# Clustered attention with a Fourier and feed-forward layer: scales in PSUM, joint sign images, the maximum's pass in place, column folds on VectorE

## The chip, the cores and the metric

The kernel runs on one core of one Trainium2 chip. A core has five engines that run their own instruction queues: TensorE (PE; its weight loads are shown as PEld), VectorE (DVE), ScalarE (ACT), GpSimd (POOL) and SyncE (SP, which issues the DMAs). The metric is the time of one execution on the device in microseconds. Before the change three runs gave 1049.66, 1053.15 and 1053.73 us; their median is 1053.15 us.

## The reference

Four sequences (batch 4) of 768 tokens, 8 heads of 64. Queries and keys are each assigned to the nearest of 16 centroids; a query attends only to keys of its own cluster. The attention's output becomes the input `x` (4 x 768 x 512) of a layer that mixes with a Fourier transform and then applies a feed-forward network.

```python
mask = q_assign[:, :, :, None] == k_assign[:, :, None, :]
scores = np.where(mask, scale * q @ k.T, -1e9)
scores = scores - np.max(scores, axis=-1, keepdims=True)
attn = np.exp(scores) / (np.sum(np.exp(scores), axis=-1, keepdims=True) + 1e-9)
x = attn @ v                                   # heads side by side: 4 x 768 x 512
mixed = np.real(np.fft.fft(np.fft.fft(x, axis=1), axis=2))
u = x + mixed
un = (u - mean(u)) / np.sqrt(var(u) + 1e-6)    # over the 512 columns
out = u + np.maximum(un @ w_ch1, 0.0) @ w_ch2  # 512 -> 2048 -> 512
```

## The kernel before

Float32 operands are split into two 16-bit parts, a high one and the rest, and each product is made of three 16-bit matmuls. So besides PE's matmuls there is much splitting work on ACT (the high part), DVE or POOL (the rest).

**Attention** (class `Attention`) goes over 16 pairs of heads, four pairs per sequence, and in each pair over six tiles of 128 queries (`scores`, then `attend` two tiles later). For one tile and each head of the pair, PE makes scores of 128 x 768 in a two-bank PSUM tile `ps_big` (L320, with the cluster mask added at L325). DVE makes one pass over them (L339): it multiplies by a column `ne` (the negative scale) and takes the minimum along the row into `m`; the product itself goes to a destination `ju`. ACT makes the exponential (L343 or L345) with `m` as its bias, casts it to 16 bit (L353), POOL subtracts for the rest (L354), a DMA transposes both (`pt`), and PE multiplies with the values into `ps_o` (L374 to L376). `finish` divides on DVE (L386 to L390) and writes into `X`, the layer's input.

Here the first sequence (four pairs, `early`) differs from the other three. In the first, the product goes to a piece of `X[1]` and the exponential reads it from there with a constant scale of -1 (L343). In the other three the product goes to a 16-bit scratch tile `ju` that nobody reads, and the exponential reads the scores again from PSUM with the scale as a column `e` (L345).

**Weights** (class `Weights`) are split once, beside the first sequence's attention. There are 32 pieces of 128 x 512, 16 for each matrix, loaded as raw bytes through eight buffers. Per piece: `largest` takes the maximum of the upper half words (DVE, L491), `signs` makes two 16-bit images with ACT, one of the positive and one of the negative values (L519, L520), `join` adds them on PE into PSUM (L528) and puts the low bits back (DVE, L532), `halve` splits into high and low part. `signs` of a piece runs one step ahead of its `join`, `largest` three steps. The PSUM tiles of `psf` are a ring of three banks that the weights share with the attention's preparation, the Fourier and the feed-forward stages. For each group of four pieces, `scales` calls `top_power`: four operations of DVE on one column (first matrix, through `block`) or four columns (second matrix), L58 to L61, which turn a maximum into a power of two `s` and its inverse `inv`. Their operands lie in SBUF.

**Fourier** (class `Fourier`): `fold` uses the symmetry of the transform. For a difference and for a sum it adds rows (L660, DVE), then mirrored columns (L661: POOL for the difference, which comes first; DVE for the sum), splits the result and transposes it by DMA. It also folds one middle row on POOL (L654, L655), which `rest` transposes on PE later (L678 to L681). `transform` makes the matmuls.

**Feed-forward** (class `FeedForward`): `norm`, `up` (L858) and `down` (L888), the largest part of PE's work.

**Order.** `Overlap.run` lists what is done in which of some hundred time steps; PE's order is the program's. The layer of sequence b runs as a generator beside the attention of sequence b + 1: `fill` takes so much of it per tile that a budget of cost is used up, and the last sequence's layer runs alone. On the other engines a planner with a model of the costs orders the instructions at build time, so their order can change wherever a cost or a dependence changes.

Of the kernel before, what the change touches and what calls it, by code (L numbers as in the profile page):

```python
# [24 lines left out]

P = 128
B, H, S, D = 4, 8, 768, 64
NC_ = 16
ST = S // P
DM = H * D  # L30
DF = 4 * DM
SH = S // 2
# [19 lines left out]
FLOOR = float(2.0 ** -38)  # L52


def top_power(nc, tops, s, inv):

    t = tops.bitcast(I32)
    nc.vector.tensor_scalar(out=t, in0=t, scalar1=20, scalar2=None, op0=ALU.logical_shift_right)  # L58
    nc.vector.tensor_scalar(out=t, in0=t, scalar1=-910.0, scalar2=1.0, op0=ALU.add, op1=ALU.max)
    nc.vector.tensor_scalar(out=inv.bitcast(I32), in0=t, scalar1=240.0, scalar2=float(1 << 23), op0=ALU.min, op1=ALU.mult)  # L60
    nc.vector.reciprocal(out=s, in_=inv)  # L61
# [20 lines left out]
class Attention:  # L82
# [226 lines left out]
    def scores(self, pr, st):  # L309
        nc, sb = self.nc, self.sb  # L310
        assert self.ready >= pr
        (hq, hk), oh, (e, ne) = self.hl[pr], self.oht[pr], self.sc.scores(pr)
        sl = slice(st * P, (st + 1) * P)
        ps = [self.psum().rearrange("p (h x) -> p h x", h=2) for _ in range(2)]
        rows = [slice(D * j, D * (j + 1)) for j in range(2)]
        for hf in range(2):
            hs = slice(hf * SH, (hf + 1) * SH)
            for i, (a, c) in enumerate(((0, 0), (1, 0), (0, 1))):
                for j in range(2):
                    nc.tensor.matmul(out=ps[j][:, hf, 0:SH], lhsT=hq[rows[j], a, sl], rhs=hk[rows[j], c, hs],  # L320
                                     start=(i == 0), stop=False)
        for hf in range(2):
            for j in range(2):
                rz = slice(D * j + 32 * hf, D * j + 32 * hf + 32)
                nc.tensor.matmul(out=ps[j][:, hf, 0:SH].rearrange("p (s x) -> p s x", x=P), lhsT=oh[rz, st % 3 * 2 + st // 3],  # L325
                                 rhs=oh[rz, ST:], start=False, stop=True)
        for j in range(2):

            m = sb.tile([P, 1], F32, name="rmx", tag="rmx", bufs=6)
            early = pr < H // 2  # L330
            if early:

                n = (2 * st + j) % self.RING * S
                p32 = self.X[1].rearrange("p a x -> p (a x)")[:, n:n + S]
            else:
                p32 = sb.tile([P, S], F32, name="p32", tag="p32", bufs=2)
            x = p32.rearrange("p (h x) -> p h x", h=2)
            ju = x if early else sb.tile([P, 2, SH], BF16, name="ju", tag="ju")
            self.mark = nc.vector.tensor_scalar(out=ju, in0=ps[j][:, :, 0:SH], scalar1=ne, scalar2=None, op0=ALU.mult, op1=ALU.min,  # L339
                                    accum_out=m)  # L340
            self.late = m
            if early:
                nc.scalar.activation(p32, p32, AF.Exp, bias=m, scale=-1.0)  # L343
            else:
                nc.scalar.activation(x, ps[j][:, :, 0:SH], AF.Exp, bias=m, scale=e)  # L345
            if early and j:
                ph = sb.tile([P, S], F32, name="p32", tag="p32", bufs=2).bitcast(F16).rearrange("p (a x) -> p a x", a=2)
            else:
                ph = sb.tile([P, 2, S], F16, name="ph", tag="ph", bufs=2)
            if early and j and (st in self.PC):  # L350
                nc.gpsimd.tensor_copy(out=ph[:, 0], in_=p32)
            else:
                nc.scalar.copy(out=ph[:, 0], in_=p32)  # L353
            nc.gpsimd.tensor_tensor(out=ph[:, 1], in0=p32, in1=ph[:, 0], op=ALU.subtract)  # L354
# [79 lines left out]
class Weights:  # L434
# [6 lines left out]

    RAW, PN = tuple(4128 * i for i in range(6)) + (29696, 33824), (24768, 26816)
    ID, TOP, MX = 28864, 29376, 29472
    X32 = 37952, 40000
    EXTRA, A2, AHEAD = 0, 9, 7

# [51 lines left out]
    def block(self, g):  # L498

        nc, at = self.nc, self.arena.at  # L500
        mx = at(self.MX + 32 * (g % 2), [P, 4], F32)
        ps = self.psf()
        along(nc, ps[:, 0:P], mx[:, 0:1], self.ident)
        nc.vector.tensor_reduce(out=mx[:, 1:2], in_=ps[:, 0:P], op=ALU.max, axis=AX.X)
        self.scales(g, mx[:, 1:2])

    def scales(self, g, mx):
        n = mx.shape[1]
        s = self.sb.tile([P, 4], F32, name="wsc", tag="wsc", bufs=2)
        top_power(self.nc, mx, s[:, 0:n], self.inv[0][:, g:g + 1] if n == 1 else self.inv[1][:, 4 * (g - 4):4 * (g - 3)])  # L510
        for i in range(4):
            self.scale[4 * g + i] = s[:, i % n:i % n + 1]

    def signs(self, k):

        nc, at = self.nc, self.arena.at
        pn = at(self.PN[k % 2], [P, 2, DM], BF16)
        top = self.top(k)
        nc.scalar.activation(pn[:, 0].bitcast(I16), top.bitcast(I16), AF.Relu, bias=self.off[:, 0:1], scale=8.0)  # L519
        nc.scalar.activation(pn[:, 1].bitcast(I16), top, AF.Relu, bias=self.off[:, 1:2], scale=8.0)  # L520
        self.bits[k] = pn
# [99 lines left out]
class Fourier:  # L621
# [8 lines left out]

    CS, SS = (33888, 30816, 20480), (35456, 32352, 22016)
    FOLDS = ((1, ALU.subtract), (0, ALU.add))
    FE = (0, 0, 0, 1)
    UE = (1, 1, 1, 1)

    def __init__(self, tc, X, arena, psf, con, ident, sc):
# [10 lines left out]
    def fold(self, b):  # L647
        nc, at, X = self.nc, self.arena.at, self.X[b % 2]
        W, M = SH + 1, DM // 2
        self.tables()  # L650
        self.scale[b] = self.sc.sequence(b)
        s = self.scale[b][0]
        mid = at(self.XM, [1, M + 1], F32)
        nc.gpsimd.tensor_copy(out=mid, in_=X[0:1, 3, 0:M + 1])  # L654
        nc.gpsimd.tensor_tensor(out=mid[:, 1:M], in0=mid[:, 1:M], in1=X[0:1, 3, DM - 1:M:-1], op=ALU.add)  # L655
        last = at(self.XL, [P, 3], F32)
        xt = {}
        for i, op in self.FOLDS:
            f = at(self.XF, [P, 3, DM], F32)
            self.engine(self.FE[i]).tensor_tensor(out=f, in0=X[:, 0:3], in1=X[:, 3:6], op=op)  # L660
            self.engine(self.FE[2 + i]).tensor_tensor(out=f[:, :, 1:M], in0=f[:, :, 1:M], in1=f[:, :, DM - 1:M:-1], op=op)  # L661
# [239 lines left out]
class Overlap:  # L901
# [21 lines left out]
    MIX3 = (0, 0, 0, 0, 0, 0, 0, 1, 1, 1)  # L923
    F2 = 1
    PIN, PF, PV = (), 29, 1
    CE, WP, WQ = 0.45, 0, 0

    def layer(self, b, old):
        fft, ffn = self.fft, self.ffn
        mix = iter(self.MIX3 if b == B - 1 else self.MIX)  # L930
        for t in fft.transform(b):
            if t == "first":
                with self.tc.high_priority():
                    m = ffn.norm(b, 0)
                ffn.inverse(*m)
                continue
            yield 0.8 if t is None else None
            for _ in range(next(mix)):
                c = next(old, 0.0)
                if c:  # L940
                    yield c
        yield from old
        for blk in range(3):
            for f, cost in enumerate(ffn.up(blk)):
                if blk == 0 and f == 0:
# [171 lines left out]
```

## Time and profile before

| | us |
|---|---|
| median of three runs | 1053.15 |
| the profiled execution | 1049.91 |
| its span (first to last instruction) | 1048.1 |
| PE busy | 910.8 (87%) |
| DVE busy | 627.4 (60%) |
| ACT busy | 625.3 (60%) |
| POOL busy | 586.9 (56%) |

Busy time is the time in which an engine has an instruction under way. A view of groups has the line, engine and operation, the output's and the input's names and shapes, the count, then busy time and the mean in ns of one, then the engine's idle time just before, with what ended it. A view of waits says which line waited for which, with the total in us, how often, and the longest. The first sequence's attention with the weights lies in about the first 220 us; the last sequence's layer, alone, in about the last 150.

### The profile page before, as it was taken

What the parts mean: (1) busy time and instruction counts of PE and PEld (TensorE: products, weight loads), DVE (VectorE), ACT (ScalarE), POOL (GpSimd) and SP (SyncE); (2) the same over time, 40 slices, a digit from 0 to 9 for tenths busy, and PEclk for the clock granted to TensorE, in tenths of its full rate; (3) what the DMA queues carried; (4) which work ended last, traced back from release to release, by engine and by line L of the source; (5) the groups of instructions that cost most, each with busy time, mean ns of one, the idle gap of its engine ahead of it and who ended that gap; (6) DMA issues with size and microseconds to landing.
All of it is one profiled execution on the core that took longest, in us unless ns stands there. A gap on an engine that the chain in (4) does not pass through costs nothing.

```text
span 1048.1 us, 23542 instructions
## 1 busy us (share of the span) xinstructions
PE 910.8 (87%) x9350; PEld 591.7 (56%) x9362; DVE 627.4 (60%) x1297; ACT 625.3 (60%) x980; POOL 586.9 (56%) x693
## 2 busy tenths in 40 slices
PE   3665565749899999998899999997999999999998
PEld 2333333425575756655666757555757667576674
DVE  8789899767757555668656555667555333631110
ACT  4798889755766665645666746556756543351230
POOL 2364565753975756655856646647847645271230
PEclk9987878769899999999899999998999999999999
DMA  7799998979887776568877767588757562321000
GB/s 272 179 225 245 196 239 166 171 156 153 177 123 153 128 154 121 121 137 161 153 137 142 140 128 132 110 141 170 124 102 133 96 110 43 81 52 31 11 11 21
DMA packets 396239, 140.01 MB, mean 134 GB/s; under 512 B 381784, under 2 KB 381792, under 8 KB 396128
## 3 DMA queue, kind: packets, MB, share of 16 engines
q1 hardware_dynamic: 396128, 138.50, 65.9%
q8 instruction: 73, 1.20, 0.5%
q14 instruction: 38, 0.31, 0.1%
HBM read 42.52 MB, written 6.29 MB: 47 GB/s over the span
## 4 chain that ended last, share of the span: by engine, by line
PE 39%; DVE 6%; DMA 3%; ACT 3%; POOL 2%; issue 2%; SPq 0%; ACTq 0%; DVEq 0%; POOLq 0%
PE ps_f L888 16%; PE ps_f L858 13%; PE ps_big L320 3%; DMA pt<-ph 3%; PE ps_f L713 2%; DVE ju L339 1%; ACT p L345 1%; PE ps_o L374 1%; POOL ph L354 1%; PE ps_o L375 1%; PE ps_o L376 1%; PE ps_big L325 1%; ACT ph L353 1%; DMA scr<-in_k_dram 0%; DVE arena L660 0%
## 5 line engine op out<-in xcount | busy, mean ns | idle before, releaser
L354 POOL TENSOR_TENSOR ph<-p,ph 128x768 f16<-128x768 f32 x144 | 242.9, 1688 | 184.6 <-ACT ph L353 150.1
L858 PE MATMUL ps_f<-arena,w1h 128*128 128x256 f16 x1536 | 271.4, 277 | 19.1 <-ACT arena L866 9.0
L888 PE MATMUL ps_f<-w2h,arena 128*128 128x512 f16 x768 | 238.9, 379 | 0.0
L345 ACT ACTIVATE p<-ps_big,rmx,sce 128x768 f32<-128x768 f32 x144 | 142.1, 988 | 132.9 <-DVE ju L339 127.5
L858 PE MATMUL ps_f<-arena,w1l 128*128 128x256 f16 x768 | 212.4, 277 | 0.0
L339 DVE TENSOR_SCALAR_CACHE_REDUCE ju<-ps_big,sce 128x768 bf16<-128x768 f32 x144 | 146.1, 1014 | 68.2 <-PE ps_big L325 58.2
L888 PEld LDWEIGHTS <-arena 128*128 128x128 f16 x1152 | 108.7, 98 | 126.6 <-issue 5.2
L858 PEld LDWEIGHTS <-w1h 128*128 128x128 f16 x1536 | 152.1, 99 | 36.0 <-issue 14.3
L867 POOL TENSOR_TENSOR arena<-arena 128x256 f16<-128x256 f32 x192 | 128.1, 677 | 77.3 <-ACT arena L866 73.6
L320 PE MATMUL ps_big<-hlk,hlq 64*128 64x384 f16 x1152 | 128.9, 348 | 39.0 <-ACT p L345 23.4
L374 PE MATMUL ps_o<-v,pt 128*128 128x66 f16 x1152 | 124.8, 198 | 43.0 <-DVE X L390 27.5
L888 PE MATMUL ps_f<-w2l,arena 128*128 128x512 f16 x384 | 145.5, 379 | 0.0
L374 PEld LDWEIGHTS <-pt 128*128 128x128 f16 x1152 | 110.2, 100 | 57.7 <-issue 37.1
L353 ACT CAST ph<-p 128x768 f16<-128x768 f32 x144 | 119.6, 832 | 15.0 <-DMA pt<-ph 12.8
L375 PE MATMUL ps_o<-v,pt 128*128 128x64 f16 x1152 | 124.8, 199 | 0.0
L376 PE MATMUL ps_o<-v,pt 128*128 128x66 f16 x1152 | 124.5, 198 | 0.0
L866 ACT ACTIVATE arena<-ps_f,wrel 128x256 f16<-128x256 f32 x192 | 90.1, 472 | 54.8 <-DVE arena L863 54.7
L863 DVE TENSOR_SCALAR arena<-ps_f,wrel 128x256 f32<-128x256 f32 x96 | 46.3, 482 | 124.9 <-PE ps_f L858 66.4
L320 PEld LDWEIGHTS <-hlq 64*128 64x128 f16 x1152 | 55.5, 99 | 101.5 <-issue 72.7
L375 PEld LDWEIGHTS <-pt 128*128 128x128 f16 x1152 | 110.7, 101 | 2.8
L376 PEld LDWEIGHTS <-pt 128*128 128x128 f16 x1152 | 111.1, 103 | 0.0
L858 PEld LDWEIGHTS <-w1l 128*128 128x128 f16 x768 | 76.1, 99 | 20.2 <-issue 10.7
(178 smaller groups left out, 1330.4 us busy)
## 6 DMA issues: line engine op xcount, KB each, us to landing
arena<-in_moe_w_ch_dram SPq DMA_DIRECT2D x32, 512.0 KB, 6.8
scr<-in_q_dram SPq DMA_DIRECT2D x16, 384.0 KB, 2.9
scr<-in_k_dram SPq DMA_DIRECT2D x16, 384.0 KB, 4.5
vst<-in_v_dram SPq DMA_DIRECT2D x16, 384.0 KB, 3.5
out_dram<-arena SPq DMA_DIRECT2D x24, 256.0 KB, 2.3
pt<-ph SPq DMA_TRANSPOSE x168, 3.9
arena<-in_cs_dram SPq DMA_DIRECT2D x12, 192.0 KB, 3.5
arena<-in_ss_dram SPq DMA_DIRECT2D x12, 192.0 KB, 3.5
```

Of the source, the lines that this page charges most:

```text
L320: nc.tensor.matmul(out=ps[j][:, hf, 0:SH], lhsT=hq[rows[j], a, sl], rhs=hk[rows[j], c, hs], start=(i == 0), stop=False)
L339: self.mark = nc.vector.tensor_scalar(out=ju, in0=ps[j][:, :, 0:SH], scalar1=ne, scalar2=None, op0=ALU.mult, op1=ALU.min, accum_out=m)
L345: nc.scalar.activation(x, ps[j][:, :, 0:SH], AF.Exp, bias=m, scale=e)
L353: nc.scalar.copy(out=ph[:, 0], in_=p32)
L354: nc.gpsimd.tensor_tensor(out=ph[:, 1], in0=p32, in1=ph[:, 0], op=ALU.subtract)
L374: nc.tensor.matmul(out=o[:, at:at + W], lhsT=hi, rhs=v16[:, kt, 0:W], start=(kt == 0), stop=False)
L375: nc.tensor.matmul(out=o[:, at:at + D], lhsT=hi, rhs=v16[:, kt, 66:130], start=False, stop=False)
L376: nc.tensor.matmul(out=o[:, at:at + W], lhsT=lo, rhs=v16[:, kt, 0:W], start=False, stop=(kt == ST - 1))
L858: nc.tensor.matmul(out=ps.rearrange("p (t x) -> p t x", x=P), lhsT=a[:, dc, fs], rhs=c[:, :, dc], start=(i == 0), stop=(i == 11))
L866: nc.scalar.activation(hh[:, f], ps, AF.Relu, scale=rel[:, f:f + 1])
L867: nc.gpsimd.tensor_tensor(out=hl[:, f], in0=r, in1=hh[:, f], op=ALU.subtract)
L888: nc.tensor.matmul(out=ps, lhsT=a[:, f, ts], rhs=c[:, f], start=(i == 0), stop=(i == 47))
```

## The change

Four parts. `top_power` gets a destination `t` apart from its input: with one column the maximum is reduced into a PSUM column and all but the last steps stay there; with four, a new tile of the three-bank ring is taken for `t`. `signs` makes the images of two pieces in one operation each, into a buffer twice as large. The three later sequences' pass over the scores writes its product back in place in PSUM, and the exponential reads that with the constant scale -1. The column fold of the difference moves from POOL to DVE, and the middle row's two POOL operations move behind the folds.

```diff
-def top_power(nc, tops, s, inv):
-    t = tops.bitcast(I32)
-    nc.vector.tensor_scalar(out=t, in0=t, scalar1=20, scalar2=None, op0=ALU.logical_shift_right)
+def top_power(nc, tops, t, s, inv):
+    t = t.bitcast(I32)
+    nc.vector.tensor_scalar(out=t, in0=tops.bitcast(I32), scalar1=20, scalar2=None, op0=ALU.logical_shift_right)
     nc.vector.tensor_scalar(out=t, in0=t, scalar1=-910.0, scalar2=1.0, op0=ALU.add, op1=ALU.max)
     nc.vector.tensor_scalar(out=inv.bitcast(I32), in0=t, scalar1=240.0, scalar2=float(1 << 23), op0=ALU.min, op1=ALU.mult)
     nc.vector.reciprocal(out=s, in_=inv)
...
-        (hq, hk), oh, (e, ne) = self.hl[pr], self.oht[pr], self.sc.scores(pr)
+        (hq, hk), oh, ne = self.hl[pr], self.oht[pr], self.sc.scores(pr)[1]
...
-            ju = x if early else sb.tile([P, 2, SH], BF16, name="ju", tag="ju")
+            ju = x if early else ps[j][:, :, 0:SH]
...
-            if early:
-                nc.scalar.activation(p32, p32, AF.Exp, bias=m, scale=-1.0)
-            else:
-                nc.scalar.activation(x, ps[j][:, :, 0:SH], AF.Exp, bias=m, scale=e)
+            nc.scalar.activation(x, ju, AF.Exp, bias=m, scale=-1.0)
...
-        nc.vector.tensor_reduce(out=mx[:, 1:2], in_=ps[:, 0:P], op=ALU.max, axis=AX.X)
-        self.scales(g, mx[:, 1:2])
+        nc.vector.tensor_reduce(out=ps[:, P:P + 1], in_=ps[:, 0:P], op=ALU.max, axis=AX.X)
+        self.scales(g, ps[:, P:P + 1])
...
+        t = self.psf()[:, 0:n] if n > 1 else mx
+        top_power(self.nc, mx, t, s[:, 0:n], ...)
...
+        if self.JOINT:
+            if k % 2 == 0:
+                pn = at(self.PN2[k // 2 % 2], [P, 2, 2, DM], BF16)
+                raw = at(self.RAW[k % len(self.RAW)], [P, 2, 4 * DM + 16], U16)
+                top = raw[:, :, 4:4 + 4 * DM].rearrange("p a (n f) -> p a n f", f=4)[:, :, :, 0]
+                nc.scalar.activation(pn[:, 0].bitcast(I16), top.bitcast(I16), AF.Relu, bias=self.off[:, 0:1], scale=8.0)
+                nc.scalar.activation(pn[:, 1].bitcast(I16), top, AF.Relu, bias=self.off[:, 1:2], scale=8.0)
+                self.bits[k], self.bits[k + 1] = pn[:, :, 0], pn[:, :, 1]
+            return
...
-    FE = (0, 0, 0, 1)
+    FE = (0, 0, 0, 0)
...
-        mid = at(self.XM, [1, M + 1], F32)
-        nc.gpsimd.tensor_copy(out=mid, in_=X[0:1, 3, 0:M + 1])
-        nc.gpsimd.tensor_tensor(out=mid[:, 1:M], in0=mid[:, 1:M], in1=X[0:1, 3, DM - 1:M:-1], op=ALU.add)
...
             xt[i] = t.rearrange("p (a t c) x -> p a t c x", a=2, t=3)
+        mid = at(self.XM, [1, M + 1], F32)
+        nc.gpsimd.tensor_copy(out=mid, in_=X[0:1, 3, 0:M + 1])
+        nc.gpsimd.tensor_tensor(out=mid[:, 1:M], in0=mid[:, 1:M], in1=X[0:1, 3, DM - 1:M:-1], op=ALU.add)
```

Two new settings, `WAIT = (0, 0)` and `N1 = 0`, keep the layer's order as it was.

More of the change, by code (lines that the diff above doesn't have):

```diff
@@ L443 @@
     ID, TOP, MX = 28864, 29376, 29472
+    JOINT, PN2 = 1, (24768, 42048)
     X32 = 37952, 40000
@@ L509, in scales @@
         s = self.sb.tile([P, 4], F32, name="wsc", tag="wsc", bufs=2)
-        top_power(self.nc, mx, s[:, 0:n], self.inv[0][:, g:g + 1] if n == 1 else self.inv[1][:, 4 * (g - 4):4 * (g - 3)])
+        t = self.psf()[:, 0:n] if n > 1 else mx
+        top_power(self.nc, mx, t, s[:, 0:n], self.inv[0][:, g:g + 1] if n == 1 else self.inv[1][:, 4 * (g - 4):4 * (g - 3)])
         for i in range(4):
@@ L925 @@
     PIN, PF, PV = (), 29, 1
+    WAIT, N1 = (0, 0), 0
     CE, WP, WQ = 0.45, 0, 0
@@ L942, in layer @@
         yield from old
+        if b < B - 1:
+            for _ in range(self.WAIT[b > 0]):
+                yield None
         for blk in range(3):
             for f, cost in enumerate(ffn.up(blk)):
-                if blk == 0 and f == 0:
+                if blk == 0 and f == self.N1:
                     ffn.inverse(*ffn.norm(b, 1))
```

## The prediction, made before the changed kernel was run

> **What bounds the kernel now.** I read the view of busy time by stretches first, because shares of the whole span hide that this kernel has several stages. Its columns are the stretch, its length, then the busy time of PE, weight load, DVE, ACT and POOL (with instruction counts), the granted clock, the DMA share and GB/s.
>
> ```profile
> 30.00:200.00 170.00, 105.59 (x1262) 61.67 (x1271) 146.35 (x295) 148.41 (x214) 99.47 (x85) 0.84 0.94 207
> 200.00:250.00 50.00, 32.85 (x350) 19.71 (x346) 35.19 (x67) 27.62 (x39) 26.70 (x22) 0.73 0.94 168
> 500.00:650.00 150.00, 145.82 (x1627) 98.97 (x1627) 88.30 (x186) 96.42 (x150) 97.82 (x116) 0.98 0.72 135
> 750.00:900.00 150.00, 146.37 (x1521) 96.50 (x1517) 66.22 (x134) 81.22 (x131) 81.60 (x89) 1.00 0.56 99
> ```
>
> From 250 us on PE is nearly always busy (145.82 of 150): there, work taken off another engine pays only where PE has a hole. The stage from 30 to 200 us, in which the weights are split beside the first sequence's attention, is different: PE works 105.59 of 170 us, while DVE (146.35, 86%), ACT (148.41, 87%) and the DMA engines (0.94) are all close to full. A microsecond gained there shifts everything behind it. Next, the waits of that stage (total us, times, longest):
>
> ```profile
> PE ps_o L374 <- DVE X L390: 27.5, 6, 5.5
> PE ps_big L320 <- DVE X L339: 14.8, 17, 3.7
> PE ps_o L374 <- DMA pt<-p: 8.2, 7, 2.6
> PE ps_o L374 <- DMA pt<-ph: 4.6, 3, 2.1
> DVE arena L491 <- DMA arena<-in_moe_w_ch_dram: 7.9, 7, 2.0
> ACT w2h L538 <- DVE ps_f L532: 5.8, 6, 2.7
> ```
>
> PE waits 42.3 us for two DVE lines and 12.8 us for transposed probabilities; ACT too waits for DVE, and DVE for the weights' DMA. So DVE sets the pace, with the DMA close behind.
>
> **Part 1: the weights' scales (L58 to L61).** Grouped by form, and two neighbours that already work in PSUM (last two rows):
>
> ```profile
> L60 DVE TENSOR_SCALAR winv<-arena 128x4 int32<-128x4 int32 x4 | 6.2, 1547 | 0.1
> L59 DVE TENSOR_SCALAR arena<-arena 128x4 int32<-128x4 int32 x4 | 4.6, 1143 | 0.1
> L58 DVE TENSOR_SCALAR arena<-arena 128x4 int32<-128x4 int32 x4 | 0.8, 211 | 0.0
> L60 DVE TENSOR_SCALAR winv<-arena 128x1 int32<-128x1 int32 x4 | 0.6, 151 | 0.1
> L408 DVE TENSOR_SCALAR ps_f<-ps_f x16: 155/170/170, 11.4 to 764.1; 128x3 int32<-128x3 int32 x16
> L410 DVE TENSOR_SCALAR scp<-ps_f x16: 150/162/164, 12.1 to 764.3; 128x3 f32<-128x3 f32 x16
> ```
>
> Four elements cannot cost 1.5 us of arithmetic. The timeline (start, length) shows what they wait for:
>
> ```profile
> 116.50 1.61 DVE L59 TENSOR_SCALAR arena<-arena 128x4 int32<-128x4 int32 x1
> 118.15 1.56 DVE L60 TENSOR_SCALAR winv<-arena 128x4 int32<-128x4 int32 x1
> 116.44 1.64 POOL L354 TENSOR_TENSOR ph<-X,ph 128x768 f16<-128x768 f32 x1 [0.41 <-DVE w2l L544]
> 118.05 1.64 POOL L354 TENSOR_TENSOR p<-X,p 128x768 f16<-128x768 f32 x1
> ```
>
> Each lasts until a POOL subtraction ends (118.11 against 118.08; 119.71 against 119.69). L408 and L410, whose source is PSUM, never exceed 170 and 164 ns in 32 instances. After the change the 128x4 form costs about 168 + 168 + 161 ns instead of 211 + 1143 + 1547: 2.40 us less, four times, is 9.6 us. The 128x1 form pays up to 17 ns (168 against 151) in three operations and gains nothing: 12 x 17 ns = 0.2 us. Net 9.4 us of DVE time. The scales now take a PSUM buffer four times from a ring of three; it is held for half a microsecond and its tenant three back has been read a step earlier, so I cost that at nothing; if that cover fails, the nearest row is PE's wait at L528 for such a buffer (4.6 us in three times, longest 2.8).
>
> The Trainium skill speaks against this edit: in "VectorE: DVE Perf Modes", section on the TRN2 errata, a fixed cost of 58 cycles is given from SBUF and 120 from PSUM. By it each operation would be some 65 ns longer (an estimate from that page at its 0.96 GHz), 1.6 us over 24, and the net 8.0 instead of 9.4. Here the rows show 17 ns.
>
> How much of the 9.4 shortens the stage? At most all; nothing if the DMA takes over. Of PE's waits above 42.3 of 55.1 (0.77) name DVE; I take two thirds, since part of what DVE gains will turn into waits such as L491's: **6.3 us**.
>
> **Part 2: sign images (L519, L520).**
>
> ```profile
> L519 ACT ACTIVATE arena<-arena 128x512 int16<-128x512 int16 x32 | 24.1, 753 | 4.6 <-PE ps_f L528 1.6 <-PE ps_o L376 1.5 <-DMA scr<-in_q_dram 1.5
> L520 ACT ACTIVATE arena<-arena 128x512 int16<-128x512 uint16 x32 | 24.0, 749 | 0.0
> L827 ACT CAST arena<-arena 128x512 f16<-128x512 f32 x24 | 13.8, 612 | 0.0
> L353 ACT CAST ph<-p 128x768 f16<-128x768 f32 x144 | 119.6, 832 | 15.0 <-DMA pt<-ph 12.8
> ```
>
> 64 operations of 512 elements (48.1 us) become 32 of 1024. L827 and L353 give (832 - 612) / 256 = 0.86 ns per element, so a joint one costs 753 + 512 x 0.86 = 1193 ns, 38.2 us in all: 9.9 less. If the 53 ns that L519 has beyond a cast and one pointer operand (0.09 us, part 3) lie in its stride and double too, 8.3. I take 9 us; the outer bounds are 0 (both halves at full price) and 9.9. The wait added: a joint operation needs the second piece's load, but L491 has already read that piece on DVE a step earlier. No wait of PE in the stage names ACT, so I pass on a quarter: **2.2 us**.
>
> **Part 3: the maximum's pass in PSUM (L339, L345).**
>
> ```profile
> L339 DVE TENSOR_SCALAR_CACHE_REDUCE ju<-ps_big,sce 128x768 bf16<-128x768 f32 x144 | 146.1, 1014 | 68.2 <-PE ps_big L325 58.2 <-ACT arena L866 2.0 <-DVE ju L339 0.9
> L345 ACT ACTIVATE p<-ps_big,rmx,sce 128x768 f32<-128x768 f32 x144 | 142.1, 988 | 132.9 <-DVE ju L339 127.5 <-POOL ph L354 5.4
> L641 ACT ACTIVATE arena<-ps_f 128x257 f16<-128x257 f32 x24 | 9.3, 388 | 15.6 <-PE ps_f L728 9.8 <-PE ps_f L713 4.1 <-DVE arena L642 1.1
> L774 ACT ACTIVATE arena<-ps_f,vseq 128x257 f32<-128x257 f32 x12 | 5.7, 471 | 6.7 <-DVE rpow L822 3.6 <-PE ps_f L763 3.1
> PE ps_big L320 <- ACT p L345: 23.4, 14, 4.3
> ```
>
> DVE's own cost stays: L408 (to PSUM) and L410 (to SBUF) differ by 7 ns, 144 times 1.0 us; bounds -1 to +1. The gain is a by-product: the exponential's scale becomes the constant -1 instead of a column. L774 (scale a column) costs 83 ns more than L641 (constant) at the same size, so L345 falls from 988 to about 905 ns: 144 x 83 ns = 12 us of ACT. Behind 250 us PE covers most of that. It shows where PE waits for the score buffer: 14 waits, each behind one exponential or two, 0.083 to 0.17 us: 1.2 to 2.4. I take **1.3 us**; bounds 0 and 2.4.
>
> **Part 4: column folds (L661) and the middle row's POOL work moved behind them.**
>
> ```profile
> L661 POOL TENSOR_TENSOR arena<-arena x4: 1805/1809/1810, 224.5 to 884.3; 128x765 f32<-128x765 f32 x4
> L661 DVE TENSOR_TENSOR arena<-arena x4: 944/1616/2277, 233.7 to 890.0; 128x765 f32<-128x765 f32 x4
> L660 DVE TENSOR_TENSOR arena<-X x8: 1748/1758/3085, 220.6 to 888.2; 128x1536 f32<-128x1536 f32 x8
> 880.62 12.95 PE ps_f L888 x60
> ```
>
> Four folds leave POOL (1.81 us each) and cost DVE 0.94 to 2.28. In the fourth, PE's chain row shows 12.95 us of L888 over the fold, so nothing is gained. In the other three DVE used POOL's time for two score passes and a split; these now come 0.94 us or more later, while the fold is ready about 0.9 us sooner. The moved copies (L654, L655) are needed only by the transposes of L678 to L681 and hide there. Bounds: 3 x (1.81 - 0.94) = 2.6 gained if the fold alone is on the path; 3 x (2.28 + the 1.33 by which L660 stretches) = 10.8 lost. I take a loss of **1 us**, near the open case.
>
> **Sum.** 6.3 + 2.2 + 1.3 - 1 = 8.8, say 9 us.
>
> ```profile
> span 1048.1 us, 23542 instructions
> ```
>
> The profiled execution took 1049.91 (span 1048.1 and 1.8 around it), so 1040.9 in its terms; it lies 3.24 under the median of the three runs, 1053.15, at their fast end. Against the median the forecast is **1044 us**.
>
> **Rivals.**
> - *The DMA becomes the bound.* At a share of 0.94 the stage cannot shrink by more than about 10 us, and transposes or weights may simply be waited for. Left is 1.3 - 1 and some part of the rest: 0 to 5 gained, about 1051. For: L491 already waits 7.9 us. Against: the weights' loads go out as DVE frees their buffers, so a faster DVE starts them sooner.
> - *Everything converts.* DVE's 9.4, ACT's 9 and 2.4 in the holes, with the fold free: 18 to 20 gained, 1034. For: most of PE's waits there end with DVE, whose work shrinks. Against: the DMA share.
> - *The scales still stall.* The third operation writes SBUF; if the write and not the source makes it wait, (1547 - 161) x 4 = 5.5 of the 9.6 stay, and the sum is 5: 1048. Against: L410 writes SBUF and never waits.
> - *Slower: the fold meets POOL.* The rows below show L660 and L661 stretched to 3.08 and 2.28 us where POOL subtracted beside them. With POOL free of its fold, the subtraction L354 starts sooner and meets three folds: 3 x 3.6 = 10.8 us on DVE, with score passes queued behind it and PE waiting for them. It ends slower by 0.5% once this loss exceeds the other gains by 5.3; with those at half (4.5), +6.3: 1059.5. Against: the shortest L661 took 0.944 us.
>
> ```profile
> 445.33 3.08 DVE L660 TENSOR_TENSOR arena<-X 128x1536 f32<-128x1536 f32 x1
> 448.45 2.28 DVE L661 TENSOR_TENSOR arena<-arena 128x765 f32<-128x765 f32 x1
> 445.04 4.87 POOL L354 TENSOR_TENSOR ph<-p,ph 128x768 f16<-128x768 f32 x2 [2.17 <-ACT ph L353]
> ```
>
> The Trainium skill has a rule for that last one: by "SBUF — State Buffer", section "SBUF: two separate sides", an operation of VectorE with two SBUF inputs and one of GpSimd exclude each other for a whole instruction. The 2277 and 3085 ns agree; the 944 ns shows it need not happen.
>
> **How the numbers follow.** Forecast 0.46, everything converts 0.12, DMA 0.24, scales still stall 0.08 (on the border, counted half to each side), slower 0.10. 0.5%, 5.3 us, is about what a measurement here tells from no change. Faster: 0.46 + 0.12 + 0.04 = 0.62; same: 0.24 + 0.04 = 0.28; slower 0.10. The range leaves out the slower case and the far end of the full conversion: 1033 to 1056.
>
> **What would show it.** Right: L59 and L60 near 165 ns; the sign operations 32 times near 1.2 us; L345 near 0.905 us; the stage from 30 to 200 us about 8 us shorter, the rest unchanged within 2. Wrong: L491's and L374's waits for DMA grown by what DVE gave up; a wait of DVE or of L528 for a PSUM buffer at the scales; L660 or L661 above 2 us in most folds; or a new order on DVE and ACT around the folds that opens holes on PE after 250 us.

## The result, and the profile after

| | median, us | range, us | runs | ratio to before, 95% interval |
|---|---|---|---|---|
| before | 1053.44 | 1049.66 to 1055.48 | 4 | |
| changed | 1063.14 | 1062.05 to 1065.33 | 4 | 1.0104, 1.0079 to 1.0128 |

The kernel became 1% slower, where 0.9% faster was forecast. In the changed kernel the line numbers move: the pass stays at L339, the exponential is L342, the first matmul with the values L371, `finish` ends at L387, the weights' maximum is L489 (its group's L494), the maximum over `along`'s result L502, the join on PE L536 and on DVE L540, the low half L552, the folds L665 and L666; on SP a piece's load is L482 and the transposes of the probabilities L353.

The profiled execution took 1065.33 us (span 1063.5). First its stretches (columns as in the prediction), then the waits of its stage from 30 to 200 us.

```profile
30.00:200.00 170.00, 102.63 (x1158) 57.61 (x1175) 133.69 (x282) 137.72 (x177) 93.38 (x80) 0.76 0.92 202
200.00:250.00 50.00, 30.21 (x381) 19.93 (x378) 39.78 (x67) 28.85 (x38) 28.37 (x23) 0.76 0.92 162
500.00:650.00 150.00, 142.22 (x1548) 93.31 (x1547) 95.53 (x192) 90.38 (x145) 101.89 (x124) 0.98 0.74 140
750.00:900.00 150.00, 146.16 (x1613) 99.90 (x1611) 69.72 (x143) 84.57 (x141) 93.64 (x109) 1.00 0.60 103
```

```profile
...
DVE arena L489 <- DMA arena<-in_moe_w_ch_dram: 19.1, 10, 4.0
ACT X L342 <- DVE X L339: 19.1, 9, 4.0
PE ps_big L320 <- DVE X L339: 17.0, 16, 3.4
...
PE ps_f L536 <- DVE w1l L552: 7.4, 3, 4.7
...
PE ps_o L371 <- DVE X L387: 6.9, 3, 6.2
...
PE ps_f L48 <- DVE winv L60: 5.3, 1, 5.3
```

In this window DVE is busy 12.7 us less (133.69 against 146.35) and ACT 10.7 us less, and still everything is later. A part of that is work that has slipped out of the window: PE makes 1158 matmuls in it instead of 1262. PE's wait for L387 fell by 20.6 us (27.5 to 6.9), as the prediction wished; in its place DVE waits 19.1 us for the weights' DMA instead of 7.9, ACT 19.1 us for the pass instead of 5.6, and PE 5.3 us at `along` (L48) for the scales' third operation (L60), a wait that the stage did not have.

The operations themselves came out as worked out. These are groups by form of the changed kernel:

```profile
L339 DVE TENSOR_SCALAR_CACHE_REDUCE ps_big<-ps_big,sce 128x768 f32<-128x768 f32 x144 | 141.5, 1020 | 45.1 <-PE ps_big L325 45.0
...
L342 ACT ACTIVATE p<-ps_big,rmx 128x768 f32<-128x768 f32 x144 | 129.0, 900 | 123.9 <-DVE ps_big L339 106.9 <-POOL ph L351 5.5 <-POOL arena L675 4.0
...
L339 DVE DVE_READ_ACCUMULATOR ps_big<-ps_big,sce 128x1 f32 x144 | 20.3, 141 | 0.0
...
L521 ACT ACTIVATE arena<-arena 128x1024 int16<-128x1024 int16 x16 | 19.5, 1219 | 5.4 <-PE ps_f L536 3.8 <-ACT v L199 0.9 <-DMA arena<-in_moe_w_ch_dram 0.7
...
L59 DVE TENSOR_SCALAR ps_f<-ps_f 128x4 int32<-128x4 int32 x4 | 0.6, 162 | 0.0
...
L58 DVE TENSOR_SCALAR ps_f<-arena 128x4 int32<-128x4 int32 x4 | 0.6, 159 | 0.0
...
L60 DVE TENSOR_SCALAR winv<-ps_f 128x4 int32<-128x4 int32 x4 | 0.6, 158 | 0.0
L60 DVE TENSOR_SCALAR winv<-ps_f 128x1 int32<-128x1 int32 x4 | 0.6, 157 | 0.1
```

The four-column scales no longer wait for POOL (159, 162 and 158 ns: 9.7 us less in all, 9.6 forecast), the joint sign image takes 1.22 us (1.19 forecast), the exponential 900 ns (905 forecast). So no operation is to blame, and the time must lie between them. Where it goes is seen best in the start of each pair's first pass at L339, read from the timeline of DVE (us, before, then differences to before in the profiled runs of the kernels that the next section explains):

| first pass of pair | before | changed | part 1 alone | its order, scales in SBUF | bank held, scales in SBUF | second matrix only |
|---|---|---|---|---|---|---|
| 0 | 31.1 | +0.1 | -0.2 | -0.5 | +0.2 | -0.5 |
| 1 | 75.9 | +7.8 | +6.3 | +5.8 | +9.2 | -0.7 |
| 2 | 125.6 | +2.6 | +1.9 | +4.5 | +11.7 | -9.1 |
| 4 | 208.5 | +5.6 | +7.0 | +8.5 | +10.0 | -3.7 |
| 5 | 264.6 | +11.0 | +8.9 | +8.5 | +10.5 | -1.1 |
| 8 | 419.0 | +16.2 | +11.1 | +10.8 | +11.7 | -0.2 |
| 12 | 642.8 | +15.2 | +12.1 | +13.4 | +11.7 | +0.7 |
| 15 | 815.1 | +15.3 | +12.1 | +13.1 | +11.9 | +0.6 |

These are single executions, and those of the kernel before spread over some 11 us (1047.7 to 1059.1), so only the larger steps are read; the two profiled executions of the kernel before and the changed one differ by 15.4 us, their medians by 9.7. All is lost by pair 8, half of it in the very first pair. The first pass of pair 2 is an exception: it can run ahead of its pair. Over the twelve passes of pair 2 the median difference is +5.2 for the changed kernel, +8.6 for part 1 alone and -2.9 for the second matrix only. The folds of the second and third sequence (between pairs 8 and 15) lose nothing.

The first pair in detail. Timeline of DVE (start, length), the changed kernel, then the kernel before at the same work:

```profile
69.02 0.69 DVE L489 TENSOR_REDUCE arena<-arena 128x1 f32<-128x512 bf16 x1 [1.08 <-DMA arena<-in_moe_w_ch_dram]
69.62 0.69 DVE L540 SCALAR_TENSOR_TENSOR ps_f<-arena,ps_f 128x512 uint32<-128x512 uint32 x1
74.26 0.69 DVE L489 TENSOR_REDUCE arena<-arena 128x1 f32<-128x512 bf16 x1 [3.96 <-DMA arena<-in_moe_w_ch_dram]
74.87 1.01 DVE L339 TENSOR_SCALAR_CACHE_REDUCE X<-ps_big,sce 128x768 f32<-128x768 f32 x1
```

```profile
66.25 0.97 DVE L339 TENSOR_SCALAR_CACHE_REDUCE X<-ps_big,sce 128x768 f32<-128x768 f32 x1
...
70.24 0.69 DVE L491 TENSOR_REDUCE arena<-arena 128x1 f32<-128x512 bf16 x1 [1.60 <-DMA arena<-in_moe_w_ch_dram]
```

Before, the pass of the last tile ran ahead of the maximum of the group's fourth piece. Now it is queued behind that maximum, which waits 3.96 us for its piece to land, and it starts 8.62 us later (74.87 against 66.25). That is an order, not a cost.

### The profile page after: what moved, and what is told of

Read it like the earlier page. It is cut to its first block, busy times and chain, and to the rows that moved or that the text cites. A ratio compares the mean times of both kernels' runs of the same rounds, so it can differ in the third digit from the quotient of the medians.

```text
span 1063.5 us, 23486 instructions
## 1 busy us (share of the span) xinstructions
PE 917.6 (86%) x9342; PEld 593.4 (56%) x9362; DVE 628.1 (59%) x1301; ACT 607.9 (57%) x948; POOL 582.6 (55%) x689
## 4 chain that ended last, share of the span: by engine, by line
PE 41%; DVE 17%; DMA 14%; ACT 10%; POOL 9%; issue 7%; SPq 1%; ACTq 0%; POOLq 0%; DVEq 0%
PE ps_f L896 16%; PE ps_f L866 14%; DMA pt<-ph 5%; DVE ps_big L339 4%; PE ps_big L320 4%; POOL ph L351 3%; DMA arena<-in_moe_w_ch_dram 3%; ACT ph L350 3%; DMA vst<-in_v_dram 2%; DVE X L339 1%; PE ps_f L721 1%; DMA pt<-p 1%; PE ps_o L371 1%; PE ps_o L373 1%; POOL arena L875 1%
## 5 line engine op out<-in xcount | busy, mean ns | idle before, releaser
L342 ACT ACTIVATE p<-ps_big,rmx 128x768 f32<-128x768 f32 x144 | 129.0, 900 | 123.9 <-DVE ps_big L339 106.9
L339 DVE TENSOR_SCALAR_CACHE_REDUCE ps_big<-ps_big,sce 128x768 f32<-128x768 f32 x144 | 141.5, 1020 | 45.1 <-PE ps_big L325 45.0
L320 PE MATMUL ps_big<-hlk,hlq 64*128 64x384 f16 x1152 | 132.4, 357 | 40.3 <-ACT p L342 21.6
L371 PE MATMUL ps_o<-v,pt 128*128 128x66 f16 x1152 | 125.7, 199 | 29.7 <-DMA pt<-p 11.7
L371 PEld LDWEIGHTS <-pt 128*128 128x128 f16 x1152 | 110.4, 100 | 44.4 <-issue 15.2
```

What stands on the lines that cost most here:

```text
L342: nc.scalar.activation(x, ju, AF.Exp, bias=m, scale=-1.0)
L371: nc.tensor.matmul(out=o[:, at:at + W], lhsT=hi, rhs=v16[:, kt, 0:W], start=(kt == 0), stop=False)
```

## The experiments

Each kernel computes the whole reference. Ratios are to runs of the kernel before on the same chip, with 95% intervals.

### One part at a time

Each keeps one part of the change and undoes the other three. The undoing of each part:

```diff
 1
-        t = self.psf()[:, 0:n] if n > 1 else mx
+        t = mx
-        self.scales(g, ps[:, P:P + 1])
+        self.scales(g, mx[:, 1:2])
...
 2
-    JOINT, PN2 = 1, (24768, 42048)
+    JOINT, PN2 = 0, (24768, 42048)
 3
...
-            ju = x if early else ps[j][:, :, 0:SH]
+            ju = x if early else sb.tile([P, 2, SH], BF16, name="ju", tag="ju")
...
-            nc.scalar.activation(x, ju, AF.Exp, bias=m, scale=-1.0)
+            nc.scalar.activation(x, ju if early else ps[j][:, :, 0:SH], AF.Exp, bias=m, scale=-1.0 if early else e)
 4
-    FE = (0, 0, 0, 0)
+    FE = (0, 0, 0, 1)
...
```

With part 1 undone the reduction of L502 writes to `mx` again, with part 3 undone the column `e` is read again, and with part 4 undone the middle row goes back ahead of the folds.

> The kernel before with part 1 alone (the scales' operations in PSUM); the planner moves 138 of DVE's 1107 instructions. Cost theory (each part does what its operations cost): the 128x4 operations fall to 165 ns, DVE loses 9.4 us of work, the time falls by 2 to 6 us (ratio 0.994 to 0.998). Order theory (the loss of the whole change comes from the planner's new orders, whatever the part): the time moves by up to 6 us either way although the operations have become cheaper. PSUM theory (the buffer that the scales take from the ring of three holds up PE's joins): waits of L536 for DVE grow, +2 to +5 us.

> The kernel before with part 2 alone (joint sign images); the planner moves 54 of DVE's instructions and 71 of ACT's 949. Cost theory: 32 operations near 1.18 us in place of 64 of 0.75, ACT loses 9 to 10 us of work, the time falls by 1 to 4 us (0.996 to 0.999). Order theory: within 4 us of before, either sign. Rival: the joint operation comes too early or too late for the loads, DVE's or ACT's waits for in_moe_w grow and the time rises by 2 to 5 us.

> The kernel before with part 3 alone (maximum's pass in place in PSUM, constant scale in the exponential); the planner moves 224 of DVE's 1107 instructions and 173 of ACT's. Cost theory: L339's accumulator read costs 58 ns more (141 against 83), the exponential 88 less; DVE gains 8 us of work behind 200 us, ACT loses 12; within 2 us of before (0.998 to 1.002). Order theory: this part moves most of the order, so most of the loss of 10 us is here: ratio 1.004 to 1.010.

> The kernel before with part 4 alone (column folds on DVE, the middle row's two POOL operations behind them); the planner moves next to nothing else (7 DVE instructions). Fold theory (the fold on DVE meets POOL's subtractions and delays the score passes): +3 to +10 us (1.003 to 1.010), L665 and L666 above 2 us in three folds of four. Order theory and cost theory: within 2 us.

| part alone | us | ratio |
|---|---|---|
| 1 scales | 1063.18 | 1.0103 (1.0070 to 1.0137) |
| 2 signs | 1054.47 | 1.0018 (0.9998 to 1.0037) |
| 3 in place | 1056.89 | 1.0037 (1.0016 to 1.0058) |
| 4 folds | 1052.48 | 0.9998 (0.9977 to 1.0019) |

Part 1, by the sum worth 6.3 us, alone loses as much as the whole change, and part 3 loses a third of that; part 4, whose meeting with POOL was the slower rival, shows no change.

Part 1 has two halves. The first matrix' 128x1 scales work in the bank that `along` filled, which so is held until L60 has read it; before, it came free at L502. The second matrix' 128x4 scales take an extra bank.

```diff
 s1_first
-        t = self.psf()[:, 0:n] if n > 1 else mx
+        t = mx
 s4_second
-        nc.vector.tensor_reduce(out=ps[:, P:P + 1], in_=ps[:, 0:P], op=ALU.max, axis=AX.X)
-        self.scales(g, ps[:, P:P + 1])
+        nc.vector.tensor_reduce(out=mx[:, 1:2], in_=ps[:, 0:P], op=ALU.max, axis=AX.X)
+        self.scales(g, mx[:, 1:2])
```

> Of part 1 only the first matrix: the 128x1 forms go to a column of the bank that along fills (four times), and the 128x4 forms of the second matrix stay in SBUF. Ring theory (held bank in the first pairs): the loss stays, 1058 to 1066, ratio 1.006 to 1.013. A rival, that the extra buffer of the ring which the 128x4 forms take is what costs: 1051 to 1055, ratio 0.998 to 1.002. Order theory gives no sign, since this kernel has an order of its own.

> Of part 1 only the second matrix: the 128x4 forms work in a buffer of the ring of three, and the first matrix' scales stay in SBUF, so that the bank of along is free at the end of L502 as in the kernel before. Ring theory: the first pair loses nothing, the 9 us of DVE that the 128x4 forms save are left, 1045 to 1051, ratio 0.993 to 0.999. Rival (the extra ring buffer costs): 1058 to 1066, ratio 1.006 to 1.013. If the two halves each lose some, the sum of s1_first and this one is near part 1's 10 us.

The first half alone: 1065.95 us, **1.0118** (1.0100 to 1.0135). The second alone: 1053.17 us, **1.0005** (0.9989 to 1.0021). So the loss comes with the held bank's half, which saves no time on any operation. The half with the extra bank loses nothing, but it saves 9.7 us of DVE and gains nothing either.

### Held bank or order

In part 1 alone PE waits for the held bank, and in the kernel before not (timelines of PE, part 1 alone, then before):

```profile
77.31 1.65 PE L48 MATMUL ps_f<-ident,amx 128*128 128x128 f32 x6 [6.13 <-DVE winv L60]
```

```profile
72.69 0.93 PE L48 MATMUL ps_f<-ident,amx 128*128 128x128 f32 x6 [0.33 <-DVE arena L504]
```

That looks like the cause: 6.13 us, and pair 1 is 6.3 us late. The rival is the planner's order, which differs on DVE, ACT and SP. That the order has to differ can be read in the kernel before:

```profile
73.67 0.57 DVE L227 TENSOR_REDUCE ps_f<-ps_f 128x3 f32<-128x384 f32 x1 [0.16 <-PE ps_f L48]
74.14 0.15 DVE L60 TENSOR_SCALAR winv<-arena 128x1 int32<-128x1 int32 x1
```

There DVE makes L227, which reads what this L48 wrote, ahead of L60. With the bank held until L60, L48 waits for L60, so L227 must come behind it. To separate hold and order, orders were written into kernels: ranks of an engine's instructions, tied one behind the other without any wait.

```diff
+def in_order(tc):
...
+    for name, table in ORDER.items():
...
+        own = [i for i in traced if str(i.engine) == "EngineType." + name and str(i.opcode) in kinds]
...
+        for a, b in zip(order, order[1:]):
+            tc.add_manual_dep(own[b], own[a].name, mybir.DependencyInfo(mybir.DependencyClass.NoSync, mybir.DependencyReason.DATA),
+                              reason="in_order")
```

> The kernel before with all its instructions, and the orders on DVE, ACT, POOL and SP replaced by those of part 1 alone (1063.18 us, ratio 1.0103). The scales stay in SBUF and take no PSUM buffer, so nothing holds a bank of ps_f longer than in the kernel before. Order theory (the loss of part 1 is the other order in which the planner put DVE's and ACT's work): 1060 to 1068, ratio 1.007 to 1.014. Ring theory (the loss is the time for which PE waits for the bank that the 128x1 scales hold until L60, 6.1 us at L48 in the first pair and 1 us in each of the other three blocks): 1050 to 1056, ratio 0.997 to 1.003.

Measured 1063.65 us, **1.0104** (1.0086 to 1.0122): the kernel before, without a single scale in PSUM, loses all of it in part 1's order. PE waits at the same place, for the reduction alone, which frees the bank as it always did:

```profile
75.80 1.65 PE L48 MATMUL ps_f<-ident,amx 128*128 128x128 f32 x6 [4.66 <-DVE arena L502]
```

It waits because L502 itself comes late. The obvious reading of the 6.13 us was wrong: the hold does not have to be there while the kernel runs. Nor is it the tying that costs: `x_p3_noneord` below has the order of the kernel before tied on four engines and is the fastest version (0.9978).

What makes the planner choose this order? One copy more holds the bank, with the scales left in SBUF:

```diff
         self.scales(g, mx[:, 1:2])
+        nc.vector.tensor_copy(out=mx[:, 1:2], in_=ps[:, 0:1])
```

> The kernel before, scales in SBUF, and one copy of 128x1 more in each of the first matrix' four blocks, which reads along's bank behind L60, so that the bank of the ring of three stays taken as long as in part 1. The planner orders anew. If the held bank is the root (joins that wait for it, loads behind the joins, an order that follows): 1058 to 1066, ratio 1.006 to 1.013. If the operands in PSUM are: 1051 to 1055, ratio 0.998 to 1.002.

Measured 1062.43 us, **1.0081** (1.0053 to 1.0108). A copy that holds the bank is enough to bring the loss, the operands in PSUM are not needed. That the hold and not the additional instruction moved the planner is likely but not shown: no kernel with a copy that leaves the bank alone was run, and orders that come without a longer hold of this bank lose too, though less (1.0027 for `x_none_s4ord`, 1.0037 for part 3). In this kernel, as in part 1, the planner puts the passes of pair 0's tile 4 behind L289, L293 and a maximum, and the load of a piece behind two transposes.

### Which part of the order

On SP the moved load is easy to see. Timeline of SP (start, time in which the queue is at that transfer), before, then part 1 alone:

```profile
56.90 1.32 SPq L484 DMA_DIRECT2D arena<-in_moe_w_ch_dram  x2
58.33 2.43 SPq L356 DMA_TRANSPOSE pt<-ph  x1
60.86 3.52 SPq L356 DMA_TRANSPOSE pt<-p  x1
...
66.30 0.33 SPq L484 DMA_DIRECT2D arena<-in_moe_w_ch_dram  x1
```

```profile
57.12 0.37 SPq L482 DMA_DIRECT2D arena<-in_moe_w_ch_dram  x1
57.69 2.82 SPq L353 DMA_TRANSPOSE pt<-ph  x1
60.67 2.44 SPq L353 DMA_TRANSPOSE pt<-p  x1
63.16 0.57 SPq L482 DMA_DIRECT2D arena<-in_moe_w_ch_dram  x1
...
68.89 0.33 SPq L482 DMA_DIRECT2D arena<-in_moe_w_ch_dram  x1
```

Before, both loads had gone out by 58.2; in part 1 the second goes at 63.16. Its piece is the third of the group, for which L489 waits 1.49 us and starts at 67.54. Behind that maximum stands the join (68.14 to 68.83) that frees the buffer of the next load, which so goes at 68.89 instead of 66.30; for its piece, the fourth, L489 waits 3.93 us until 72.76. The changed kernel shows the same chain (loads at 64.37 and 70.33, maxima at 69.02 and 74.26). Five kernels take the order apart: the four passes of tiles 4 and 5 of pair 0 moved back (`x_p1_move`) or, in the kernel before, moved late (`x_before_late`); SP's order alone (`x_b_sp`); and part 1 with much of the old order (`x_p1_noneord`, `x_p1_sp_move`). The whole old order is not possible in part 1's code: DVE, with L227 ahead of L60, and PE, with L48 behind L60, would wait for each other.

> Part 1 alone, with the order of the kernel before imposed on ACT, POOL and SP, and on DVE for all but the weights' own operations (L489, L494, L502, L58 to L61, L540, L552), which the planner places freely. Order theory: the loss goes and the 6 us that the shorter scales save are left, 1045 to 1053, ratio 0.993 to 1.000. Ring theory: PE still waits for the held banks, 1060 to 1066, ratio 1.007 to 1.013.

> Part 1 alone in its own order on DVE, ACT, POOL and SP, but for four passes of L339 on DVE: the two of pair 0's step 4 stand right behind L285 again and the two of step 5 right behind L385, as in the kernel before, no longer behind L489's wait for a piece of the weights. Scales still in PSUM, bank of along still held until L60. If these four places make the loss of the first pair (6.3 us at pair 1's first pass): pair 1 starts at 75 to 78 instead of 82.2, and the time is 1054 to 1059, since another 4 to 6 us are lost later, in an order that stays part 1's. If the held bank makes it (6.1 us of PE at L48): pair 1 at 81 to 83 and 1061 to 1065.

> The kernel before in its own order, but for the same four passes, which are moved to where part 1's order has them: step 4's two behind L289, L293, the maximum and the halving that follow, step 5's two behind the maximum that waits for its piece. Nothing else changes. If the four places make the loss: pair 1 starts 5 to 7 us later (81 to 83) and the time is 1055 to 1060. If not: pair 1 at 76 to 77, 1051 to 1055.

> The kernel before, with its own order on DVE, ACT and POOL; on SP the order of part 1, in which ten of 389 transfers stand elsewhere, first the load of a weights' piece behind two transposes of pair 0 instead of ahead of them. If SP's order carries the loss: pair 1's first pass 4 to 6 us late, 1058 to 1064, ratio 1.005 to 1.011. If DVE's and ACT's orders carry it: 1050 to 1055, ratio 0.998 to 1.003.

> Part 1 alone with SP's order of the kernel before and the four passes of L339 where the kernel before has them; the rest of DVE, ACT and POOL in part 1's order, scales in PSUM, bank of along held until L60. If the late load and the passes are the loss of the first pairs: pair 1 at 75 to 78, 1050 to 1057, ratio 0.998 to 1.005. If the held bank or the rest of DVE's and ACT's order: pair 1 at 80 to 82, 1058 to 1064.

| kernel | us | ratio | pair 1 starts |
|---|---|---|---|
| x_p1_noneord | 1068.65 | 1.0156 (1.0133 to 1.0179) | 85.3 |
| x_p1_move | 1061.40 | 1.0097 (1.0079 to 1.0116) | 81.3 |
| x_before_late | 1055.53 | 1.0034 (1.0019 to 1.0050) | 79.1 |
| x_b_sp | 1064.84 | 1.0115 (1.0088 to 1.0143) | 78.4 |
| x_p1_sp_move | 1072.15 | 1.0191 (1.0163 to 1.0220) | 83.2 |

The four passes explain a third when made late, and next to nothing when moved back, where L489 still waits until 73.47 us for its piece and `along` with it. SP's order alone in the kernel before reproduces the size of the loss, though not its places: it loses 2.5 us at pair 1 and 13.2 at pair 2's third tile. But giving SP its old order back in part 1 does not help; it loses most of all. The waits of SP's queue for the joins (40 to 130 us; total, times, longest) point to the reason. Before; part 1 alone; SP's order of part 1 in the kernel before; SP's old order in part 1:

```profile
SPq L484 <- DVE ps_f L532: 8.9, 6, 2.9
```

```profile
SPq L482 <- DVE ps_f L540: 15.0, 7, 5.3
```

```profile
SPq L482 <- DVE ps_f L540: 15.2, 5, 5.6
```

```profile
SPq L482 <- DVE ps_f L540: 20.3, 6, 8.7
```

A load needs the buffer that a join has read; while it waits at the head of SP's queue, nothing behind it goes: in part 1 SP waits 3.7 us for a join ahead of the load at 68.89, and the transpose behind it goes at 69.33. An order of SP that fits one order of joins on DVE need not fit another. So no single queue carries the loss: every mixture of the two orders lost. Which of its steps weighs how much stays open.

Another remedy is to trace each step of the weights behind the latest pass (part 1 alone, with one constant changed):

```diff
-    CE, WP, WQ = 0.45, 0, 0
+    CE, WP, WQ = 0.45, 0, 1
```

> Part 1 alone, with each step of the weights traced behind the latest pass of L339 on DVE (the constant WQ set to 1), so that no maximum that waits for its piece stands ahead of a pass traced before it; the planner orders anew. If waits of L489 ahead of the passes are the cause in all pairs, and not in the first alone: 1045 to 1054. If the order matters in ways that this rule does not reach, or the held bank: 1058 to 1066.

Measured 1056.06 us, **1.0049** (1.0032 to 1.0067), between both theories: pair 1 starts at 75.2, and the waits between 20 and 220 us have no row left of L489 waiting for a piece, but 4.1 us are lost again by pair 5.

### Costs with the order held fixed

Two kernels change operations and keep an order. `x_p3_noneord` is part 3 in the order of the kernel before; `x_none_s4ord` has the scales of before in the order of `s4_second`.

> Part 3 alone (the maximum's pass writes its product back into PSUM from pair 4 on and the exponential reads it there) in the order of the kernel before on every engine. Order theory: the loss of p3_inplace (1.0037) is its order, and with the old one the operations' own costs are left: 144 exponentials shorter by 88 ns and 144 accumulator reads longer by 58 ns, 1050 to 1053, ratio 0.997 to 1.000. Cost theory (the longer accumulator read, 144 x 58 ns = 8.4 us of DVE, is the loss): 1055 to 1059, ratio 1.003 to 1.006.

> The kernel before with its scales in SBUF, in the order that the planner gave s4_second (128x4 scales in PSUM, 1.0005) on DVE, ACT, POOL and SP. Its difference to s4_second is what the shorter 128x4 scales bring with the order fixed. If their 9.4 us of DVE convert to two thirds as predicted: 1057 to 1061, ratio 1.005 to 1.008. If transfers set the end of the stage and the saving is hidden: 1051 to 1055, ratio 0.999 to 1.003.

Part 3: 1050.17 us, **0.9978** (0.9960 to 0.9996), 2.3 us faster; in the planner's own order it was 1.0037. This is the only version measured that beats both kernels. Shorter 128x4 scales: 1.0027 (1.0007 to 1.0048; 1056.34 us) falls to 1.0005, some 2.3 us, and the intervals overlap. These two kernels do not differ by 9.7 us of DVE, since in this order the scales in SBUF wait less for POOL. `x_none_s4ord` by form:

```profile
L59 DVE TENSOR_SCALAR arena<-arena 128x4 int32<-128x4 int32 x4 | 2.9, 720 | 0.0
...
L60 DVE TENSOR_SCALAR winv<-arena 128x4 int32<-128x4 int32 x4 | 2.2, 548 | 0.0
L58 DVE TENSOR_SCALAR arena<-arena 128x4 int32<-128x4 int32 x4 | 2.0, 489 | 0.0
```

That is 1757 ns against 456 in `s4_second` (154, 162 and 140), 5.2 us for four times, in one execution each; so some 2.3 of 5.2 us came through, which the noise does not settle. By the medians over a pair's twelve passes, `s4_second` is 4.0 us ahead of `x_none_s4ord` in pair 2, 2.7 in pair 3 and 1.8 at the end: the lead shrinks. The 9.1 us by which its first pass of pair 2 is ahead of the kernel before say little, as `x_none_s4ord` already has 5.8 there.

The waits of `s4_second` in pair 2 (116.5 to 166 us), and those of the kernel before in its pair 2 (125.6 to 170.9):

```profile
...
PE ps_o L371 <- DMA pt<-ph: 9.0, 3, 6.7
...
PE ps_o L371 <- DMA pt<-p: 6.2, 5, 2.4
...
PE ps_o L371 <- DVE X L387: 2.1, 1, 2.1
```

```profile
...
PE ps_o L374 <- DVE X L390: 10.2, 2, 5.5
...
PE ps_o L374 <- DMA pt<-ph: 2.0, 1, 2.0
...
PE ps_o L374 <- DMA pt<-p: 1.6, 2, 1.2
```

PE's wait for DVE is 8.1 us shorter (2.1 against 10.2), and it waits 15.2 us for transposed probabilities instead of 3.6. But `x_none_s4ord` shows nearly the same in its pair 2 (119.8 to 167.5 us): 2.0 us for DVE and 12.7 for transposes. So this exchange comes with the order, and 2.5 us more of it with the shorter scales. The DMA share in pair 2 is 0.97 in `s4_second`, 0.91 in `x_none_s4ord` and 0.99 before; that the DMA takes back the lead is a reading of these waits, not a test.

### The other parts together

> The changed kernel with part 1 undone: joint signs, in place, folds, and the scales in SBUF as before. Sum of the single parts (1.0018, 1.0037, 0.9998): 1.005, 1058. If each part's loss is that of one bad order, which the parts together don't add: between 1050 and 1060. Prediction's costs (2.2 and 1.3 gained, 1 lost): 1050 to 1051.

> The whole change, but the first matrix' scales in SBUF as before, so that along's bank is free at the end of L502; joint signs, in place, folds and the 128x4 scales in PSUM as changed. If the held bank is the whole loss: near m1_scales (1.0045) or below it, 1048 to 1057, ratio 0.997 to 1.005. If any order of these parts loses like part 1's: 1058 to 1066.

`m1_scales` undoes part 1 in the changed kernel, `s4_all` only its first half (the edit of `s4_second`). Without part 1: 1055.83 us, **1.0045** (1.0023 to 1.0066). With part 1's second half only: 1060.95 us, **1.0072** (1.0046 to 1.0098), an interval that overlaps with those of both the whole change and `m1_scales`. So freeing the bank is not enough once the other parts have their own orders, and the losses do not add up: 1.0103 for part 1 and 1.0045 for the rest make 1.0104 together. Why they don't is open. For the whole change the order is the cause by inference: its first pair has the places of part 1's order, but neither its operations in another order nor its order with the operations of before were run.

## Why the prediction was wrong

- **The step that failed** is in part 1: a ring of three that loses nothing, "so I cost that at nothing". It looked at the new bank that the 128x4 form takes; there no loss came (`s4_second`, 1.0005). It did not look at the 128x1 form, which "gains nothing" by the prediction and seemed to cost 0.2 us: it holds `along`'s bank from L502 to L60. The price it named for a failing cover, a wait at the join of 4.6 us, was of the wrong kind too. The loss is not a wait for the bank but the order in which the planner then puts the work: that order costs 1.0104 without any hold (`x_none_p1ord`), and a copy that holds the bank brings 1.0081 (`h_hold`). In place of 6.3 us gained, part 1 alone lost some 10.5.
- **No term for new orders.** More generally, the sum prices each part's operations in the old order. For part 3 the planner's order turns a gain of 2.3 us into a loss of 3.9.
- **Two thirds of 9.4 us as gain** is not confirmed: with the order fixed, 5.2 us of DVE brought about 2.3 (two thirds would be 3.5), and the noise does not tell these apart. The rival "the DMA becomes the bound" fits the waits for transposes in `s4_second`, but its time (1051) was covered by the loss and it stays untested.
- **Part 2**: duration right, but 2.2 us of gain (0.9979) lies outside the measured 0.9998 to 1.0037. Here the order was not held fixed, so what the shorter operations bring by themselves is open.
- **Part 3**: right. 1.3 us was forecast and 2.3 measured with the order fixed, within the interval. PE's wait for the score buffer behind the exponential is 21.4 us there instead of 23.4, 14 times in both, as it reckoned. One term was wrong without effect: DVE's own cost was to stay within 1 us, but the accumulator read that follows each pass grew by 8.4 us in all (last section).
- **Part 4**: right at -1 us within the interval, which holds no change too. The slower rival (the fold meets POOL) falls: single folds reach 2.76 us, but the part alone is at 0.9998, and the changed kernel loses no time between pairs 8 and 15, where two folds lie. (The profiled execution of part 4 alone, 1056.03 us, one of its slower ones, does lose 3.9 us from pair 8 to pair 9; `x_b_sp`, without part 4, loses 4.1 there.)
- **"The scales still stall"** falls: 158 ns at L60, which writes SBUF.
- **The rule** that the Trainium skill gives for PSUM operands ("VectorE: DVE Perf Modes", section on the TRN2 errata), 65 ns more for each operation by the estimate, does not show here: L60's 128x1 form took 157 ns from PSUM and 151 from SBUF.
- **The signs named** were the right ones: grown DMA waits of L491, and a wait for a PSUM buffer at the scales, though at L48 and not at DVE or L528. A new order was named too, but placed at the folds behind 250 us; half of the loss lay in the first pair.
- **A slip without effect** in part 2: what L519 has beyond a cast and a pointer operand is 753 - 612 - 83 = 58 ns, not 53, which makes 8.1 us and not 8.3.

The granted clock is no rival for the cause: it fell to 0.76 in the stage (0.84 before), but `s4_second` had 0.76 between 30 and 208 us and a span of 1049.1.

## What to carry to other kernels

Where a planner orders the queues, ask of each edit not only what its operations cost but which buffer it holds longer, and who is next in that ring: half of an edit that saves nothing can reorder a whole stage. Test an edit's cost with the old order imposed, and its order with the old operations; the two can have opposite signs (0.9978 and 1.0037 for one part). In a stage in which DVE, ACT and DMA are all near full, less than half of what DVE saved seems to have come back (2.3 of 5.2 us, not clear of the noise). And when an order is imposed, measure the operations again: here the same scales took 2.9 us in one order and 1.8 in another.

## What the hardware showed besides

Reading the accumulator takes longer when the pass writes PSUM: 141 ns, against this row of the kernel before.

```profile
L339 DVE DVE_READ_ACCUMULATOR ju<-ps_big,sce 128x1 f32 x144 | 11.9, 83 | 0.0
```

In the changed kernel's timeline of DVE the next operation starts beside it:

```profile
435.18 1.02 DVE L339 TENSOR_SCALAR_CACHE_REDUCE ps_big<-ps_big,sce 128x768 f32<-128x768 f32 x1
436.11 0.14 DVE L339 DVE_READ_ACCUMULATOR ps_big<-ps_big,sce 128x1 f32 x1
436.11 1.02 DVE L236 SCALAR_TENSOR_TENSOR hlq<-scr,scp,hlq 128x768 f16<-128x768 f32 x1
```

The 58 ns more, 144 times, would be 8.4 us on DVE; `x_p3_noneord` has them too (141 ns) and is faster than the kernel before, so no loss from them shows.
